# Whole transfers for the first K, the first wq pair, the last dwq pair and the last dV and dK, and a four-rows-a-partition layout for the last wo and dwo

## The chip, the cores and the metric

The kernel runs on one core of a Trainium2 chip. The metric is device time in microseconds (us), the median of several runs. The core has a matrix engine (TensorE, PE in the profile; its weight loads are PEld), a vector engine (VectorE, DVE), a scalar engine (ScalarE, ACT), GpSimd (POOL) and SyncE (SP), which here only issues transfers. Sixteen DMA engines move all data between the device memory and the on-chip memory, whose 128 rows are called partitions.

## What is computed

The forward pass is one decode step, and the kernel returns its output and the gradients of all its inputs but one:

```
q = (x @ wq) per head (32 heads of 128);  s = q . K / sqrt(128);  p = softmax(s)
a = (p @ V, heads side by side) @ wo
h = x @ w1 + b1;  b = (h * tanh(softplus(h))) @ w2
out = g * a + (1 - g) * b,   g = sigmoid(sum(x * gate_w))
returned: out, dx, dK, dV, dwq, dwo, dw1, db1, dw2, dgate_w     (for a given grad_out)
```

x has 640 elements, K and V are 32 x 4096 x 128, wq is 640 x 4096, wo is 4096 x 640, w1 is 640 x 1728, w2 is 1728 x 640, all in bf16. For each head, dV is the outer product of p with the gradient of that head's output, and dK the outer product of ds with the scaled q. So 64 MB of K and V are read, and as much of dK and dV is written.

## The kernel before

The work is a loop over the 32 heads, in groups of four (G = 4, NG = 8 groups). One head's K is one tile of 128 partitions x 32 rows x 128 elements: each partition holds 32 consecutive rows of the cache, 8192 bytes that lie together in device memory. Per head the kernel transposes K and V on TensorE (`k_tr`, `v_tr`, L504, with ScalarE copying the result at L505), computes the scores and dP (L510), the softmax (`softmax`, `exps`, `probs`), the two sums for dq and o (`dq_o`, L592), and on VectorE the two outer products into `o_sb` tiles (`outer`, L569), four of which rotate. `dv_out` and `dk_out` call `out_pair`, which issues the 1 MB store of such a tile at L582. For the last head (h = H - 1) `out_pair` stores each half of a tile as soon as it is computed (L580).

Per group there is more: the group's rows of wq (`q` needs them, and dx) and of wo (needed for the gradient of the heads' outputs, and for a), and their gradients dwq and dwo, which are written into the same tiles as the weights and stored. The tile `wq_p` holds a pair of groups, 640 rows as 128 partitions x 5 x 1024 columns. Loaded in one transfer (`load_wqp`, L130) its pieces are 2048 bytes, loaded by one group (`load_wqh`, L126) they are 1024 bytes. Before, the first pair is loaded as two halves, around the other first loads, and the last pair's dwq is stored as two halves (`f_dwq_st`, L369); the pairs between go whole (L130, L372).

The tile `wo_g` holds a group's 512 rows of wo. For groups 0 to 6 partition p holds the rows 4p to 4p+3 (`wo4_v`), 5120 bytes that lie together. There the heads' output has to be brought into that order: `f_diag` builds `o_sel` (L287), `f_o4` multiplies it with a selection matrix on TensorE (L298) and copies the result (L299, L300), and only then can a's part (`f_aT_pe`) and dwo (`f_dwo`, L376) be computed, for the whole group at once. On the way in, `g_dodiag` spreads the column by one instruction (L269), `g_dobc` broadcasts it, and `g_docol` turns the row into columns by four small matmuls (L240). For the last group (LG = 7) the layout is `wo_v`: partition d holds row d of each of the four heads, four pieces of 1280 bytes. No reordering is needed there, and each head stands by itself, so that after the loop dwo of the first three heads is computed and stored early (`f_dwo_st(g, 0, 3)`, L382), and that of head 31 later.

What sets the order: the kernel is scheduled by hand, so each engine runs its instructions in the order of the code. SP issues all large loads and stores in one stream, from one queue. The transfers of SP and of ScalarE's queue share eight semaphores; an issue on one of them waits for the transfer that had that semaphore before. In front of the loop SP issues first K (its first half), wq of group 0, K's second half, wo of group 0, V of head 0, K 1, V 1, K 2, wq of group 1, wo of group 1, V 2, K 3, w1, w2. In the loop each head issues the stores of dK of the head before and of its own dV, and the loads of K four and V three heads ahead. Behind the loop stand the last head, dK of head 30, dwo, dwq, dV of head 31, the small outputs from ScalarE's and GpSimd's queues (L842 to L844), and dK of head 31 last.

Of the kernel before, what the change touches and what calls it, by code (L numbers as in the profile page):

```python
# [7 lines left out]
ACT = mybir.ActivationFunctionType  # L8
ALU = mybir.AluOpType
AX = mybir.AxisListType  # L10
F32 = mybir.dt.float32
BF16 = mybir.dt.bfloat16
# [4 lines left out]
def kernel(  # L17
# [24 lines left out]
    nc = tc.nc  # L42
    P = 128
    _, H, Sk, Dh = A_k_cache.shape
# [3 lines left out]
    J = Sk // P  # L48
    RC = D // P
    G = 4  # L50
    NG = H // G
    GD = G * Dh
# [7 lines left out]
    scale = float(Dh) ** -0.5  # L60
    TB = 8
    NTB = J // TB
    JH = J // 2
    W = 32

    Kv = A_k_cache.rearrange("b h (p j) d -> (b h) p j d", p=P)
# [2 lines left out]
    dVv = out_3.rearrange("b h (p j) d -> (b h) p j d", p=P)  # L69
    wq_v = A_wq.rearrange("(rc r) c -> r rc c", r=P)  # L70
    dwq_v = out_4.rearrange("(rc r) c -> r rc c", r=P)
    wo_v = A_wo.rearrange("(h d) n -> d h n", d=P)
    dwo_v = out_5.rearrange("(h d) n -> d h n", d=P)
    wo4_v = A_wo.rearrange("(g p t) n -> g p t n", p=P, t=4)
    dwo4_v = out_5.rearrange("(g p t) n -> g p t n", p=P, t=4)
    assert G == 4 and NG % 2 == 0
    LG = NG - 1
    w1_v = B_w1.rearrange("(rc r) f -> r rc f", r=P)
    dw1_v = out_6.rearrange("(rc r) f -> r rc f", r=P)
    w2_v = B_w2[0:FM, :].rearrange("(p fc) n -> p fc n", p=P)  # L80
# [14 lines left out]
    kv_in = ctx.enter_context(tc.tile_pool(name="kv_in", bufs=KBUFS))  # L95
# [10 lines left out]
    kts, vts, wqs, wos = {}, {}, {}, {}  # L106

    def load_k(h):
        if h < H:
            kts[h] = kv_in.tile([P, J, Dh], BF16, name="Kn", tag="Kn")  # L110
            nc.sync.dma_start(kts[h][:], Kv[h])
# [5 lines left out]

    wqp = {}

    def wq_pair(k):  # L120
        wqp[k] = wts.tile([P, RC, 2 * GD], BF16, name="wq_p", tag="wq_p", bufs=2)
        for i in range(2):
            wqs[2 * k + i] = wqp[k][:, :, i * GD:(i + 1) * GD]

    def load_wqh(g):
        nc.sync.dma_start(wqs[g], wq_v[:, :, g * GD:(g + 1) * GD])  # L126

    def load_wqp(k):
        wq_pair(k)
        nc.sync.dma_start(wqp[k][:], wq_v[:, :, 2 * k * GD:2 * (k + 1) * GD])  # L130

    def load_wo(g):
        wos[g] = wts.tile([P, G, D], BF16, name="wo_g", tag="wo_g")
        nc.sync.dma_start(wos[g][:], wo4_v[g] if g < LG else wo_v[:, g * G:(g + 1) * G, :])

    vec_rows = const.tile([3 * RC, P], BF16, name="vec_rows")
    nc.scalar.dma_start(vec_rows[0:RC, :], x_rows)
# [1 line left out]
    nc.scalar.dma_start(vec_rows[2 * RC:3 * RC, :], gw_rows)  # L139
    dy_sb = const.tile([1, D], BF16, name="dy_sb")  # L140
    nc.scalar.dma_start(dy_sb[:], dy_row)
    kts[0] = kv_in.tile([P, J, Dh], BF16, name="Kn", tag="Kn")
    for c in range(2):
        nc.sync.dma_start(kts[0][:, c * JH:(c + 1) * JH, :], Kv[0][:, c * JH:(c + 1) * JH, :])
        if c:
            load_wo(0)
        else:
            wq_pair(0)
            load_wqh(0)
    load_v(0)  # L150
    load_k(1)
    load_v(1)
    load_k(2)
    load_wqh(1)
    load_wo(1)
    load_v(2)
    load_k(3)
# [30 lines left out]
    aT_acc = const.tile([P, RC], F32, name="aT_acc")  # L188
# [4 lines left out]
    qz, doz, p4b, ds4b = [], [], [], []  # L193
# [38 lines left out]
        nc.vector.tensor_copy(qz[g % 2][:, :, J - 1], ps[:])  # L232

    def g_docol(g):
        if g == LG:
            nc.vector.tensor_copy(doz[g % 2][:, :, J - 1], groups[g]["do_col"][:])
            return
        ps = grp([P, G], F32, "doc_ps")
        for hh in range(G):
            nc.tensor.matmul(ps[:, hh:hh + 1], lhsT=groups[g]["do_row"][0:1, hh * Dh:(hh + 1) * Dh],  # L240
                             rhs=ones_bf[0:1, 0:1], start=True, stop=True)
        nc.vector.tensor_copy(doz[g % 2][:, :, J - 1], ps[:])
# [7 lines left out]
    def g_diag(src, sc, a, b):  # L250
        diag = grp_sb.tile([P, G, P], BF16, name="diag", tag="diag")
        for hh in range(a, b):
            nc.vector.tensor_scalar(diag[:, hh, :], ident_bf[:], src[:, hh:hh + 1], sc, ALU.mult, ALU.mult)
        return diag
# [7 lines left out]

    def g_dodiag(g):
        gp = groups[g]
        if g == LG:
            gp["do_diag"] = g_diag(gp["do_col"], 1.0, 0, G)
            return
        gp["do_diag"] = grp_sb.tile([P, G, P], BF16, name="diag", tag="diag")
        nc.vector.tensor_tensor(gp["do_diag"][:].rearrange("p h d -> p (h d)").rearrange("p (k t) -> p k t", t=4),  # L269
                                ident_bf[:].unsqueeze(2).to_broadcast([P, P, 4]),  # L270
                                gp["do_col"][:].unsqueeze(1).to_broadcast([P, P, 4]), ALU.mult)

    def g_dobc(g):
        g_bcast(groups[g]["do_diag"], groups[g]["do_row"], 0, G)
# [5 lines left out]

    def f_diag(g, a=0, b=G):
        gp = groups[g]
        if g == LG:
            nc.vector.tensor_copy(gp["o_bf"][:, a:b], gp["dqo"][:, 1, a:b])
        else:
            gp["o_sel"] = grp_sb.tile([P, G, P // 4], F32, name="o_sel", tag="o_sel")
            nc.vector.tensor_tensor(gp["o_sel"][:], seg[:].unsqueeze(1).to_broadcast([P, G, P // 4]),  # L287
                                    gp["dqo"][:, 1, :].unsqueeze(2).to_broadcast([P, G, P // 4]), ALU.mult)
        gp["dq_diag"] = g_diag(gp["dqo"][:, 0, :], scale, a, b)

    def f_bc(g, a=0, b=G):
        g_bcast(groups[g]["dq_diag"], groups[g]["dq_bc"], a, b)

    def f_o4(g):
        gp = groups[g]
        gp["o4"] = grp_sb.tile([P, G], F32, name="o4", tag="o4")
        ps = grp([P, G], F32, "o4_ps")
        nc.tensor.matmul(ps[:], lhsT=gp["o_sel"][:].rearrange("p h k -> p (h k)"), rhs=res[:], start=True, stop=True)  # L298
        nc.vector.tensor_copy(gp["o4"][:], ps[:])  # L299
        nc.vector.tensor_copy(gp["o_bf"][:], gp["o4"][:])  # L300
# [37 lines left out]
    def l_dqbf(a, b):  # L338
        gp = groups[NG - 1]
        nc.vector.tensor_scalar(gp["dq_bf"][:, a:b], gp["dqo"][:, 0, a:b], scale, None, ALU.mult)  # L340

    def l_pe(a, b):
        gp = groups[NG - 1]
        gp["ax"] = grp([P, 2, RC], F32, "ax_ps")
        for i in range(2):
            for c in range(RC):
                for hh in range(a, b):
                    nc.tensor.matmul(gp["ax"][:, i, c:c + 1],
                                     lhsT=wqT[0][:, hh * RC + c, :] if i else wos[NG - 1][:, hh, c * P:(c + 1) * P],
                                     rhs=gp["dq_bf" if i else "o_bf"][:, hh:hh + 1],  # L350
                                     start=(hh == a), stop=(hh == b - 1))

    def l_add(slot):
        ax = groups[NG - 1]["ax"]
        nc.vector.tensor_tensor(aT_acc[:], aT_acc[:], ax[:, 0, :], ALU.add)
        nc.vector.tensor_copy(dx_parts[:, :, slot], ax[:, 1, :])

    def l_dwq(c, a, b):
# [6 lines left out]
        nc.vector.tensor_scalar(wqs[g][:, c, cs], groups[g]["dq_bc"][:, cs], x_col_f[:, c:c + 1], None, ALU.mult)  # L365

    def f_dwq_st(g):
        if g >= NG - 2:
            nc.sync.dma_start(dwq_v[:, :, g * GD:(g + 1) * GD], wqs[g])  # L369
        elif g % 2:  # L370
            k = g // 2
            nc.sync.dma_start(dwq_v[:, :, 2 * k * GD:2 * (k + 1) * GD], wqp[k][:])  # L372

    def f_dwo(g, hh):
        o = groups[g]["dqo"][:, 1, :] if g == LG else groups[g]["o4"][:]
        nc.scalar.activation(wos[g][:, hh, :], da_bc[:], ACT.Copy, scale=o[:, hh:hh + 1])  # L376

    def f_dwo_st(g, a=0, b=G):
        if g < LG:
            nc.sync.dma_start(dwo4_v[g], wos[g][:])  # L380
        else:
            nc.sync.dma_start(dwo_v[:, g * G + a:g * G + b, :], wos[g][:, a:b, :])  # L382

    h_sb = const.tile([P, FCN], F32, name="h_sb")
    u_sb = const.tile([P, FCN], F32, name="u_sb")
# [188 lines left out]
    def out_pair(h, dst, col4, row):  # L574
        hh = h % G
        t = outs.tile([P, J, Dh], BF16, name="o_sb", tag="o_sb")
        for a in (0, JH):
            outer(t, col4, row[:, hh * Dh:(hh + 1) * Dh], a, a + JH)
            if h == H - 1:
                nc.sync.dma_start(dst[h][:, a:a + JH, :], t[:, a:a + JH, :])  # L580
        if h < H - 1:
            nc.sync.dma_start(dst[h], t[:])  # L582

    def dv_out(h):
        out_pair(h, dVv, p4s[h], groups[h // G]["do_row"])
# [95 lines left out]
    for h in range(H - 1):  # L681
# [7 lines left out]
        v_tr(h, 2)  # L689
        v_tr(h, 3)  # L690
        exps(h, negM)
        if hh == 0 and g == LG:
            g_dobc(g)
        dP(h)
        if hh == 0 and pv:
            f_o4(g - 1)
# [62 lines left out]
        if hh == 3:  # L759
            if g % 2 == 0 and g + 2 < NG:  # L760
                load_wqp(g // 2 + 1)
            if g + 2 < NG:
                load_wo(g + 2)
            if nx:
                if g + 1 < LG:
                    g_dobc(g + 1)
                g_q(g + 1)
                g_qs(g + 1)
                g_docol(g + 1)
                f_new(g)  # L770
                f_diag(g)
            budget = 2.7
# [26 lines left out]
    dk_out(h - 1)  # L799
    od = dq_o(h)  # L800
    l_add(g)
    for i in range(3):
        f_dwo(g, i)
    f_dwo_st(g, 0, 3)
    dqo_red(h, od)
    f_diag(g, 3, 4)
    l_dqbf(3, 4)
    f_bc(g, 3, 4)
    l_pe(3, 4)
    for c in range(RC):  # L810
# [1 line left out]
    for c in range(RC):  # L812
        l_dwq(c, 3, 4)
    f_dwq_st(g)
    f_dwo(g, 3)
    f_dwo_st(g, 3, 4)
    l_add(NG)
    fin = const.tile([P, 3 * RC], F32, name="fin")
    nc.vector.scalar_tensor_tensor(fin[:, 0:RC], in0=aT_acc[:], scalar=g_all[:], in1=gb[:], op0=ALU.mult, op1=ALU.add)
# [56 lines left out]
```

## Time and profile before

| What | Value |
|---|---|
| median of 3 runs | 416.1 us (415.33 to 416.12) |
| the profiled execution | 416.13 us, its span 414.4 us |
| TensorE busy | 317.4 us (77%) |
| VectorE busy | 301.2 us (73%) |
| ScalarE busy | 215.7 us (52%) |
| moved by DMA | 165.05 MB, on the mean 398 GB/s over the span |
| packets of SP's queue | 30866, 164.05 MB |
| packets of instruction fetch (queues 8 and 14) | 66, 0.98 MB |

The span is the time from the first to the last record of the profile; 1.7 us of the execution lie outside it. A transfer is cut into packets, one for each run of bytes that lies together on both sides. A transfer over 128 partitions gives eight partitions to each of the sixteen DMA engines, and its semaphore is raised sixteen times, once by each engine when its share has landed. The trace keeps the start, size and duration of every packet, and the time of every such raise.

### The profile page before, as it was taken

The numbers are of one execution on the slowest core, as the hardware profiler recorded it, in microseconds if no ns is written. First come the engines' busy times: TensorE is split into PE (matmuls) and PEld (weight loads), VectorE is DVE, ScalarE is ACT, GpSimd is POOL, SyncE is SP. The second block draws the span as 40 slices with busy tenths as digits, with TensorE's granted clock in tenths as the row PEclk, the third lists the DMA queues.
The fourth block names the chain that finished last, engine by engine and source line by source line (L and its number), as shares of the span: only waits on it lengthen the run. The fifth ranks groups of instructions, "written<-read, shape, count | busy, mean of one in ns | idle before, by whom it ended". The sixth has DMA issues, their size and how long they took to land.

```text
span 414.4 us, 15457 instructions
## 1 busy us (share of the span) xinstructions
PE 317.4 (77%) x6839; PEld 285.2 (69%) x6839; DVE 301.2 (73%) x811; ACT 215.7 (52%) x447; POOL 10.4 (3%) x27
## 2 busy tenths in 40 slices
PE   4697995979859988888987876787978687879400
PEld 3497874878758886878777865777778685878400
DVE  2555872888689696999898885749899996886720
ACT  2364553755446445564567654774656445546600
POOL 3000001000000000000000002000000000000000
PEclk9998998989969798898989998987989898689855
DMA  8999999999999999999999999999999999999694
GB/s 273 406 413 422 419 422 422 407 420 419 421 421 420 418 419 421 411 420 419 422 420 423 416 404 411 409 417 423 422 416 375 411 394 414 403 391 377 278 346 168
DMA packets 31240, 165.05 MB, mean 398 GB/s; under 512 B 3012, under 2 KB 6725, under 8 KB 15174
## 3 DMA queue, kind: packets, MB, share of 16 engines
q1 hardware_dynamic: 30866, 164.05, 97.3%
q8 instruction: 53, 0.87, 0.8%
q14 instruction: 13, 0.11, 0.1%
q0 software_dynamic: 256, 0.01, 0.0%
q10 hardware_dynamic: 52, 0.01, 0.0%
HBM read 82.03 MB, written 82.03 MB: 396 GB/s over the span
## 4 chain that ended last, share of the span: by engine, by line
PE 32%; DMA 30%; DVE 17%; ACT 13%; issue 4%; DVEq 0%; ACTq 0%; SPq 0%
PE tr L504 14%; DMA out_dram<-o_sb 13%; DMA Vn<-in_A_v_cache_dram 10%; PE od L592 7%; DVE o_sb L569 6%; ACT KT L505 6%; DMA out_dram<-wo_g 5%; ACT VT L505 4%; PE DP L510 2%; PE S L510 2%; DVE junk L464 2%; PE q_ps L218 2%; DMA h_sb<-dh_bc 1%; DMA Kn<-in_A_k_cache_dram 1%; DVE junk L247 1%
## 5 line engine op out<-in xcount | busy, mean ns | idle before, releaser
L505 ACT COPY KT<-tr 128x512 f32<-128x512 f32 x128 | 69.8, 588 | 54.2 <-PE tr L504 54.1
L504 PE MATMUL tr<-ident_bf,Vn 128*128 128x128 bf16 x1024 | 80.3, 239 | 17.8 <-ACT VT L505 12.5
L504 PEld LDWEIGHTS <-Vn 128*128 128x128 bf16 x1024 | 71.8, 108 | 25.5 <-issue 20.1
L569 DVE TENSOR_TENSOR o_sb<-qs_row,ds 128x2048 bf16<-128x2048 bf16 x64 | 75.3, 1217 | 17.1 <-DMA out_dram<-o_sb 17.1
L505 ACT COPY VT<-tr 128x512 f32<-128x512 f32 x128 | 69.6, 584 | 27.4 <-PE tr L504 26.9
L504 PE MATMUL tr<-ident_bf,Kn 128*128 128x128 bf16 x1024 | 75.7, 230 | 7.0 <-DMA Kn<-in_A_k_cache_dram 5.5
L504 PEld LDWEIGHTS <-Kn 128*128 128x128 bf16 x1024 | 68.1, 105 | 12.0 <-DMA Kn<-in_A_k_cache_dram 5.5
L569 DVE TENSOR_TENSOR o_sb<-do_row,p 128x2048 bf16<-128x2048 bf16 x64 | 75.2, 1216 | 0.0
L532 ACT ACTIVATE dgm<-ident_bf,m 128x128 f32<-128x128 bf16 x32 | 12.9, 402 | 57.1 <-DVE m L530 57.1
L510 PE MATMUL DP<-doz,VT 128*128 128x32 bf16 x1024 | 36.3, 178 | 4.5 <-issue 2.1
L510 PE MATMUL S<-qz,KT 128*128 128x32 bf16 x1024 | 37.1, 180 | 3.1 <-ACT KT L505 0.4
L510 PEld LDWEIGHTS <-VT 128*128 128x128 bf16 x1024 | 31.7, 97 | 7.9 <-ACT VT L505 5.1
L510 PEld LDWEIGHTS <-KT 128*128 128x128 bf16 x1024 | 32.5, 98 | 6.5 <-ACT KT L505 5.6
L592 PE MATMUL od<-p,Vn 128*128 128x32 bf16 x1024 | 31.7, 179 | 3.7 <-issue 3.7
L554 PE MATMUL mx<-zd,ones_f 128*128 128x2 f32 x64 | 12.0, 258 | 25.9 <-DVE pj L550 25.7
L592 PEld LDWEIGHTS <-Vn 128*128 128x128 bf16 x1024 | 28.7, 97 | 4.1 <-issue 4.1
L592 PE MATMUL od<-ds,Kn 128*128 128x32 bf16 x1024 | 31.3, 180 | 0.1
L554 PEld LDWEIGHTS mx<-zd,ones_f 128*128 128x128 f32 x64 | 10.0, 197 | 28.8 <-DVE pj L550 28.8
L592 PEld LDWEIGHTS <-Kn 128*128 128x128 bf16 x1024 | 28.6, 98 | 0.2 <-issue 0.2
L247 DVE SCALAR_TENSOR_TENSOR junk<-wo_g,da_bc 128x640 bf16<-128x640 bf16 x32 | 25.4, 818 | 0.0
L318 DVE SCALAR_TENSOR_TENSOR junk<-wq_p,dq_bc 128x512 bf16<-128x512 bf16 x35 | 23.4, 684 | 0.7 <-ACT dq_bc L261 0.7
L538 DVE TENSOR_REDUCE negM<-mx 128x1 f32<-128x128 f32 x32 | 9.2, 286 | 17.5 <-PE mx L536 17.4
(162 smaller groups left out, 318.4 us busy)
## 6 DMA issues: line engine op xcount, KB each, us to landing
out_dram<-o_sb SPq DMA_DIRECT2D x62, 1024.0 KB, 17.5
Vn<-in_A_v_cache_dram SPq DMA_DIRECT2D x32, 1024.0 KB, 18.6
Kn<-in_A_k_cache_dram SPq DMA_DIRECT2D x31, 1024.0 KB, 17.1
wo_g<-in_A_wo_dram SPq DMA_DIRECT2D x8, 640.0 KB, 19.2
out_dram<-wo_g SPq DMA_DIRECT2D x7, 640.0 KB, 18.3
wq_p<-in_A_wq_dram SPq DMA_DIRECT2D x3, 1280.0 KB
out_dram<-wq_p SPq DMA_DIRECT2D x3, 1280.0 KB, 21.3
w_sb<-in_B_w_dram SPq DMA_DIRECT2D x1, 2160.0 KB
```

Source lines behind the costliest of these rows:

```text
L218: nc.tensor.matmul(ps[:], lhsT=x_col_bf[:, rc:rc + 1].to_broadcast([P, P]), rhs=wqs[g][:, rc, :], start=(rc == 0), stop=(rc == RC - 1))
L247: nc.vector.scalar_tensor_tensor(junk[:], in0=wos[g][:, hh, :], scalar=1.0, in1=da_bc[:], op0=ALU.mult, op1=ALU.mult, accum_out=gp["do_col ...
L318: nc.vector.scalar_tensor_tensor(junk[:, cs], in0=wqs[g][:, c, cs], scalar=1.0, in1=gp["dq_bc"][:, cs], op0=ALU.mult, op1=ALU.mult, accum_ ...
L464: nc.vector.scalar_tensor_tensor(junk[0:n, :], in0=w2_sb[0:n, fc, :], scalar=dm[0:n, fc:fc + 1], in1=db_bc[0:n, :], op0=ALU.mult, op1=ALU. ...
L504: nc.tensor.transpose(tp[:, t, :], src[:, c * TB + t, :], ident_bf[:])
L505: nc.scalar.copy(dst[:, sl, :].rearrange("p a b -> p (a b)").bitcast(F32), tp[:].rearrange("p a b -> p (a b)").bitcast(F32))
L510: nc.tensor.matmul(out, lhsT=T[:, j, :], rhs=zrow[:, J - 1 - j:2 * J - 1 - j], start=(j == 0), stop=(j == J - 1))
L532: nc.scalar.activation(dgms[h][:], ident_bf[:], ACT.Copy, scale=m32[:])
L538: nc.vector.tensor_reduce(negM[:], mx[:, 0:P], axis=AX.X, op=ALU.max, negate=True)
L554: nc.tensor.matmul(mx[:, P:P + 2], lhsT=ones_f[:], rhs=zds[h][:], start=True, stop=True)
L569: nc.vector.tensor_tensor(dst[:, a:b, :].rearrange("p j (k t) -> p j k t", t=4), row.rearrange("p (k t) -> p k t", t=4).unsqueeze(1).to_br ...
L592: nc.tensor.matmul(out, lhsT=N[:, j, :], rhs=c4[:, 4 * j:4 * j + W], start=(j == 0), stop=(j == J - 1))
```

## The change

The first K, the first wq pair, the last dwq pair, and dV and dK of head 31 are each moved in one transfer. wo and dwo of the last group take the layout of the other groups (four consecutive rows on a partition), with the reordering that goes with it: dwo of all four heads is computed and stored once, behind the last head's sums. `load_wqh`, `wo_v`, `dwo_v` and LG are gone. For the last group `g_dobc` moves to where the other groups have it, the end of the group before.

```
+    def load_wqp(k):
         wqp[k] = wts.tile([P, RC, 2 * GD], BF16, name="wq_p", tag="wq_p", bufs=2)
...
+        nc.sync.dma_start(wqp[k][:], wq_v[:, :, 2 * k * GD:2 * (k + 1) * GD])
...
-        nc.sync.dma_start(wos[g][:], wo4_v[g] if g < LG else wo_v[:, g * G:(g + 1) * G, :])
+        nc.sync.dma_start(wos[g][:], wo4_v[g])
...
-    kts[0] = kv_in.tile([P, J, Dh], BF16, name="Kn", tag="Kn")
-    for c in range(2):
-        nc.sync.dma_start(kts[0][:, c * JH:(c + 1) * JH, :], Kv[0][:, c * JH:(c + 1) * JH, :])
-        if c:
-            load_wo(0)
-        else:
-            wq_pair(0)
-            load_wqh(0)
+    load_k(0)
+    load_wqp(0)
+    load_wo(0)
     load_v(0)
     load_k(1)
     load_v(1)
     load_k(2)
-    load_wqh(1)
     load_wo(1)
...
     def f_diag(g, a=0, b=G):
         gp = groups[g]
-        if g == LG:
-            nc.vector.tensor_copy(gp["o_bf"][:, a:b], gp["dqo"][:, 1, a:b])
-        else:
+        if b == G:
             gp["o_sel"] = ...
...
     def l_pe(a, b):
+        for c in range(RC):
+            for hh in range(a, b):
+                nc.tensor.matmul(gp["ax"][:, 1, c:c + 1], lhsT=wqT[0][:, hh * RC + c, :], rhs=gp["dq_bf"][:, hh:hh + 1], ...)
+        if b == G:
             for c in range(RC):
+                for t in range(G):
+                    nc.tensor.matmul(gp["ax"][:, 0, c:c + 1], lhsT=wos[NG - 1][:, t, c * P:(c + 1) * P], ...)
...
     def f_dwq_st(g):
-        if g >= NG - 2:
-            nc.sync.dma_start(dwq_v[:, :, g * GD:(g + 1) * GD], wqs[g])
-        elif g % 2:
+        if g % 2:
...
         for a in (0, JH):
             outer(t, col4, row[:, hh * Dh:(hh + 1) * Dh], a, a + JH)
-            if h == H - 1:
-                nc.sync.dma_start(dst[h][:, a:a + JH, :], t[:, a:a + JH, :])
-        if h < H - 1:
-            nc.sync.dma_start(dst[h], t[:])
+        nc.sync.dma_start(dst[h], t[:])
...
     l_add(g)
-    for i in range(3):
-        f_dwo(g, i)
-    f_dwo_st(g, 0, 3)
     dqo_red(h, od)
     f_diag(g, 3, 4)
     l_dqbf(3, 4)
+    f_o4(g)
     f_bc(g, 3, 4)
     l_pe(3, 4)
...
     f_dwq_st(g)
-    f_dwo(g, 3)
-    f_dwo_st(g, 3, 4)
+    for t in range(G):
+        f_dwo(g, t)
+    f_dwo_st(g)
     l_add(NG)
```

More of the change, by code (lines that the diff above doesn't have):

```diff
@@ L71 @@
     dwq_v = out_4.rearrange("(rc r) c -> r rc c", r=P)
-    wo_v = A_wo.rearrange("(h d) n -> d h n", d=P)
-    dwo_v = out_5.rearrange("(h d) n -> d h n", d=P)
     wo4_v = A_wo.rearrange("(g p t) n -> g p t n", p=P, t=4)
@@ L76 @@
     assert G == 4 and NG % 2 == 0
-    LG = NG - 1
     w1_v = B_w1.rearrange("(rc r) f -> r rc f", r=P)
@@ L118 @@
     wqp = {}
-    def wq_pair(k):
+    def load_wqp(k):
         wqp[k] = wts.tile([P, RC, 2 * GD], BF16, name="wq_p", tag="wq_p", bufs=2)
@@ L123, in wq_pair @@
             wqs[2 * k + i] = wqp[k][:, :, i * GD:(i + 1) * GD]
[L125 to L129, printed above, removed]
         nc.sync.dma_start(wqp[k][:], wq_v[:, :, 2 * k * GD:2 * (k + 1) * GD])
@@ L234, in g_docol @@
     def g_docol(g):
-        if g == LG:
-            nc.vector.tensor_copy(doz[g % 2][:, :, J - 1], groups[g]["do_col"][:])
-            return
         ps = grp([P, G], F32, "doc_ps")
@@ L264, in g_dodiag @@
         gp = groups[g]
-        if g == LG:
-            gp["do_diag"] = g_diag(gp["do_col"], 1.0, 0, G)
-            return
         gp["do_diag"] = grp_sb.tile([P, G, P], BF16, name="diag", tag="diag")
@@ L282, in f_diag @@
         gp = groups[g]
-        if g == LG:
-            nc.vector.tensor_copy(gp["o_bf"][:, a:b], gp["dqo"][:, 1, a:b])
-        else:
+        if b == G:
             gp["o_sel"] = grp_sb.tile([P, G, P // 4], F32, name="o_sel", tag="o_sel")
@@ L344, in l_pe @@
         gp["ax"] = grp([P, 2, RC], F32, "ax_ps")
-        for i in range(2):
-            for c in range(RC):
[L347 to L351, printed above, removed]
+        for c in range(RC):
+            for hh in range(a, b):
+                nc.tensor.matmul(gp["ax"][:, 1, c:c + 1], lhsT=wqT[0][:, hh * RC + c, :], rhs=gp["dq_bf"][:, hh:hh + 1],
+                                 start=(hh == a), stop=(hh == b - 1))
+        if b == G:
+            for c in range(RC):
+                for t in range(G):
+                    nc.tensor.matmul(gp["ax"][:, 0, c:c + 1], lhsT=wos[NG - 1][:, t, c * P:(c + 1) * P],
+                                     rhs=gp["o_bf"][:, t:t + 1], start=(t == 0), stop=(t == G - 1))
     def l_add(slot):
         ax = groups[NG - 1]["ax"]
-        nc.vector.tensor_tensor(aT_acc[:], aT_acc[:], ax[:, 0, :], ALU.add)
+        if slot == NG:
+            nc.vector.tensor_tensor(aT_acc[:], aT_acc[:], ax[:, 0, :], ALU.add)
         nc.vector.tensor_copy(dx_parts[:, :, slot], ax[:, 1, :])
@@ L374, in f_dwo, with f_dwo_st @@
     def f_dwo(g, hh):
[L375 to L382, printed above, removed]
+        nc.scalar.activation(wos[g][:, hh, :], da_bc[:], ACT.Copy, scale=groups[g]["o4"][:, hh:hh + 1])
+    def f_dwo_st(g):
+        nc.sync.dma_start(dwo4_v[g], wos[g][:])
     h_sb = const.tile([P, FCN], F32, name="h_sb")
@@ L691 @@
         exps(h, negM)
-        if hh == 0 and g == LG:
-            g_dobc(g)
         dP(h)
@@ L764 @@
             if nx:
-                if g + 1 < LG:
-                    g_dobc(g + 1)
+                g_dobc(g + 1)
                 g_q(g + 1)
```

## The prediction

> **What bounds the kernel.** I read the page's shares first. No compute engine is busy over 77% of the span, while the DMA row stands at 9 tenths in nearly every slice. These lines of the page say so, and that SP's queue carries nearly all of it:
>
> ```profile
> PE 317.4 (77%) x6839; PEld 285.2 (69%) x6839; DVE 301.2 (73%) x811; ACT 215.7 (52%) x447; POOL 10.4 (3%) x27
> DMA  8999999999999999999999999999999999999694
> q1 hardware_dynamic: 30866, 164.05, 97.3%
> q8 instruction: 53, 0.87, 0.8%
> ```
>
> The head and the tail are where the change acts, so next I asked for the end in short windows (columns: PE, PEld, DVE, ACT, POOL busy, granted clock, DMA share, GB/s), and for the chain of waits from 379 us on:
>
> ```profile
> 388.00:390.00 2.00, 0.45 (x11) 0.35 (x10) 1.97 (x11) 0.49 (x2) 0.00 (x0) 0.97 0.09 32
> 390.00:399.00 9.00, 0.83 (x3) 0.59 (x3) 6.31 (x17) 2.32 (x7) 0.56 (x1) 0.50 1.02 404
> 399.00:403.00 4.00, 0.00 (x0) 0.00 (x0) 0.00 (x0) 0.00 (x0) 0.00 (x0) 0.50 0.75 259
> 403.00:408.00 5.00, 0.00 (x0) 0.00 (x0) 0.00 (x0) 0.00 (x0) 0.00 (x0) 0.50 1.02 404
> 408.00:413.00 5.00, 0.00 (x0) 0.00 (x0) 0.00 (x0) 0.00 (x0) 0.00 (x0) 0.50 0.07 28
> ```
>
> ```profile
> 379.42 15.35 DMA out_dram<-o_sb
> 394.77 0.02 issue
> 394.79 1.23 DVE o_sb L569
> 396.01 1.14 DVEq L871
> ```
>
> The chain ends with VectorE at 397.2 us, but the span runs to 414.4: the last 17 us are transfers alone. In the last five of them the share is 0.07, about one sixteenth, at 28 GB/s. One DMA engine is working, and fifteen are done.
>
> That engine is found in the landings, the sixteen semaphore raises of a transfer (us):
>
> ```
> transfer            issued   first  15th    last
> K 0, first half      0.74     4.18    5.41    5.43
> K 4                 28.39    43.30   45.51   45.53
> K 16               156.78   164.74  169.61  172.29
> V 30               348.35   356.17  360.74  369.69
> dK 30              392.35   398.23  398.41  405.26
> dK 31, second half 403.74   408.37  408.54  413.45
> ```
>
> One engine falls behind as the run goes on, by 9 us at 370. Listing the last landings in order of issue, each stands after the one before by what its bytes take. From dK 30: 405.26, 406.49, 408.10, 408.49, 409.75, 410.97, 412.21, 413.45. The last five steps are 0.39 (160 KB) and 1.22 to 1.26 (512 KB), and eight packets of 4096 bytes that start 0.155 apart make 1.24. So the last engine has no gap, not even at 388 to 390 us where the others sit at a share of 0.09. **The end is the last engine's stream of packets**, plus 0.9 us to the span's end (414.36) and 1.77 outside. The instruction fetches (53 of 16 KB, 1.03 us each beside other packets) are the likeliest reason that it lags, which only affects the forecast if it changes.
>
> **The change by what this stream carries.** One packet's share of the stream is its median duration less 3.5 ns, since 4096-byte packets of 159 ns start 155 apart. In ns: 1024 bytes 42.3 (46), 1280 bytes 51.5 (55), 2048 bytes 80.5 (84), 4096 bytes 155.3, 5120 bytes 192.5 (196), 8192 bytes 305.5 (309). Each engine has a sixteenth of a transfer's packets.
> - wq and dwq: four halves of 40 packets, 160 x 42.3 = 6.77 us, become two pairs of 40, 80 x 80.5 = 6.44. **-0.33.**
> - wo and dwo of group 7: 64 x 51.5 = 3.30 become 16 x 192.5 = 3.08. **-0.22.**
> - K 0, dV 31, dK 31: 48 x 155.3 = 7.45 become 24 x 305.5 = 7.33. **-0.12.**
> - Six transfers fewer, each with one semaphore packet of 7 to 9 ns: **-0.04.**
>
> The sum is **-0.7 us**. From the profiled 416.13 that gives 415.4; the runs' median 416.1 is the same within 0.03.
>
> The bounds of this term. Low: the last engine's own steps over the wq halves were 1.82, 1.80, 1.70 and 1.61, 6.93 in all, and over whole pairs 3.33 to 3.47 where no fetch shows, so two pairs may cost 6.94 and save nothing; with the other terms at their floor the saving is some 0.3. High: by mean durations, traffic included (48.9, 57.8, 86.0, 164.7, 200.4, 316.4 ns, less 3.5), wq saves 0.66, wo 0.33 and the halves 0.23, with the semaphores 1.25 in all. I take the medians because the tail, where most of these packets run, ran at them.
>
> A fixed cost of each transfer is not in the sum, because the four half stores land 1.22 to 1.26 apart and their packets alone make 1.24. The Trainium skill, "DMA: Bandwidth & Descriptors", section "Anatomy of one DMA — SWDGE (gpsimd) path", gives some 2.0 us fixed per DMA besides its bytes (for GpSimd's path). If that stood in this stream, six fewer would save 12 us; the trace disagrees.
>
> **The head, edit by edit.** K 0's halves landed at 5.43 and 8.63 with the wq half between (7.25). Whole, K 0 lands at 5.43 + 1.3 = 6.7, the wq pair at 6.7 + 3.3 = 10.0. TensorE's first transposes (5.47) wait 1.3 longer. Its queue holds behind them the matmuls on wq (L230, 7.75), and behind those the gate's z_ps, the broadcast of dy, and all of head 0; VectorE's g_do and the first store wait for these. wq now comes at 10.0, so all this moves by about 2.5 us: da_bc to 13.2, V 0's transposes from 19.1 to 21.6, the first store from 27.94 to 30.4. What hides it is the queue: when SP issued that store, the loads before it were still to land until 40.74, and at its next store (35.58) until 48.01. The least cover is 12.4 us, against 2.5. K 0's ramp is unpriced: its first packet starts at 1.75 and its last engine lands at 5.43, 3.7 us where eight packets make 1.24, so the ramp is 2.4. If it goes with bytes, the second half costs up to 2.4 more; if it is chance which engine pays, the last one may come off as well as the first (4.18), 1.25 less. I take zero, since wq's 1024-byte packets ran at about 50 ns at once behind it, near their 46.
>
> **In the loop.** The last group's four diag instructions (0.73 in all) become one of 0.68; four doc_ps matmuls (0.16 each) and the broadcast run a head earlier. wq 1 comes with wq 0. None is on the DMA stream. The half store of dwq at 375.09 goes: the stream behind it, dV 30 and dK 29 included, is 1.7 us earlier, and dK 31's outer products, which waited for the tile of dK 29 (394.77), start sooner.
>
> **The tail.** VectorE gets o_sel (0.28) and two copies (0.16 + 0.17) and loses two casts and an add; TensorE gets one product (about 0.5 with both passes), on which o_bf, the last ax_ps and aT_acc wait, and behind them on VectorE dV 31's outer products: +0.7 us at about 389. ScalarE's four dwo pieces (0.81 each) now all follow l_dwq, ready at 391.35: dwo complete at 394.5. fin_rows behind them may slip 0.5. SP then has dwq, dwo, dV 31, dK 31, all computed by about 397. Behind the semaphores of the small outputs, which held the dwq half until 398.85, they are issued by some 401. The last engine finishes dK 30 at 405.26 - 1.7 = 403.5 and reaches dK 31 near 410. All are hidden by its backlog, with over 2 us to spare at the tightest. If that cover were gone and the other fifteen engines set the end: a transfer issued into an idle queue (dw1, 389.04) first landed at 393.56 with 24 packets of 134 ns, so it started some 1.3 us after its issue. dwq issued at 398.85 would give 400.2 + 3.3 + 1.6 + 4.9 = 410.0, against their 408.5 now: 1.5 worse, still before 412.8.
>
> **The rivals.**
> 1. Forecast: only the packets count, 415.4, its own range 415.2 to 415.9. Chance 0.50.
> 2. Larger saving: traffic widens small packets as in the means (-1.25), and the wo load's step of 2.32 us, 0.66 over its work, shrinks or K 0's ramp does too: 414.8. For it: 1024-byte packets averaged 48.9, not 46. Against: the tail's ran at 46. Chance 0.27.
> 3. Slower, the head: the 2.5 us of later compute reach the end. It decides if the queue runs dry before the first stores, that is if the 12.4 us of cover are used up. Price: 2.5 - 0.7, time 417.9. The Trainium skill's same page, in the rules for kernel authors, asks to issue early and overlap compute with the transfer; by that rule the halves help. The trace has them hidden here. Against: five times the cover. K 0's ramp by bytes (+2.4 - 0.7) ends at nearly the same time, 417.8. Chance 0.13.
> 4. Nothing gained: the last engine's other delays (some 20 us over its bare packets, steps of 0.5 to 1.6 at fetches) shift by as much as is saved: 416.1. Chance 0.09.
> 5. Each transfer pays a start of its own, as K 0 paid 2.4 us: six fewer save 14.4 besides the packets, 401.0. Against: the half stores' steps. Chance 0.01. By the skill's 2.0 us it would be 403.4.
>
> **Chances.** This kernel's measurement can tell about 0.2%, 0.83 us, from no change. Faster by more: rivals 2 and 5 and little of 1, 0.30. Within: most of 1 and rival 4, 0.55. Slower: rival 3 and some of 4, 0.15. The range runs from the forecast with K 0's luckier ramp (415.4 - 1.25), below rival 2, to short of rival 3: 414.2 to 417.2.
>
> **What would show it.** Right: the last five us again at a DMA share near 0.07, last landing near 412.8, steps of 3.3 at pairs and 2.45 at dV 31 and dK 31. First store near 30.4 with no DMA slice under 9 before 60 us. Wrong: a DMA hole between 25 and 50 us (rival 3), all sixteen engines ending together (no lag, so the tail's order counts), or a last engine with gaps behind dK 30.

## The result and the profile after

The changed kernel takes 417.2 us (median of 10 runs, 416.17 to 418.53), the one before 415.54 (10 runs, 415.25 to 416.12). The ratio is 1.0039, with a 95% interval of 1.0024 to 1.0054: slower by 1.6 us, where 0.7 us faster was forecast. 417.2 is at the top edge of the stated range. The profiled execution took 417.09 us, its span is 415.3.

The page after, in the lines that were shown of before:

```profile
PE 318.2 (77%) x6845; PEld 284.4 (68%) x6845; DVE 303.3 (73%) x808; ACT 216.1 (52%) x447; POOL 11.4 (3%) x27
DMA  8999999999999999999999999999999999999892
GB/s 289 419 417 420 421 412 419 397 360 415 421 417 354 389 412 409 414 417 420 423 418 424 421 413 425 410 420 420 420 425 419 417 399 412 419 392 400 333 381 85
q1 hardware_dynamic: 28338, 164.05, 96.9%
q8 instruction: 53, 0.87, 0.8%
```

SP's queue moves the same bytes in 2528 packets fewer, and the row of tenths is as full as before. The rate tells more than the tenths. It falls in two places where it had not: 360 GB/s in the ninth slice (83 to 93 us) and 354 in the thirteenth (125 to 135). In the page of before the same two slices have 420:

```profile
GB/s 273 406 413 422 419 422 422 407 420 419 421 421 420 418 419 421 411 420 419 422 420 423 416 404 411 409 417 423 422 416 375 411 394 414 403 391 377 278 346 168
```

The end, in windows (columns: PE, PEld, DVE, ACT, POOL busy, granted clock, DMA share, GB/s), and the chain of waits from 395 us on:

```profile
403.00:408.00 5.00, 0.00 (x0) 0.00 (x0) 0.00 (x0) 0.00 (x0) 0.00 (x0) 0.50 0.76 311
408.00:414.00 6.00, 0.00 (x0) 0.00 (x0) 0.00 (x0) 0.00 (x0) 0.00 (x0) 0.50 0.06 25
```

```profile
395.92 1.12 DVEq L838
397.04 1.13 DVE o_sb L543
```

This is as forecast: the outer products are done at 398.2, and in the last six us one DMA engine works alone. Its last landings from dK 30 on are 404.53, 407.66 (dwq pair), 409.20 (dwo), 411.63 (dV 31), 414.05 (dK 31), steps of 3.13, 1.54, 2.43 and 2.42 that hold nothing but packets.

So the loss came earlier. The last engine's landing of the same transfers in the two traces:

```
                       before    after    difference
tail of w2 (last of    40.74     39.83    -0.91
 the first loads)
V 9                   116.25    116.15    -0.11
V 11                  138.61    141.29    +2.68
V 31                  377.49    378.49    +1.00
last dK               413.45    414.05    +0.60
```

The first loads arrived 0.9 us sooner. Between them and V 31 the stream lost 1.9, and behind V 31 it won 0.4 back. In this execution the net is +0.6 us at the last landing; over all runs it is +1.6. The path between is not a straight one: at V 11 the last engine is 2.68 behind, and by V 31 it has made up 1.7 of that. Each column is one execution, and the last engine takes delays of its own in both.

### The profile page after: what moved, and what is told of

The parts are those of the page before. It is cut to its first block, busy times and chain, and to the rows that moved or that the text cites. A ratio compares the mean times of both kernels' runs of the same rounds, so it can differ in the third digit from the quotient of the medians.

```text
span 415.3 us, 15457 instructions
## 1 busy us (share of the span) xinstructions
PE 318.2 (77%) x6845; PEld 284.4 (68%) x6845; DVE 303.3 (73%) x808; ACT 216.1 (52%) x447; POOL 11.4 (3%) x27
## 4 chain that ended last, share of the span: by engine, by line
PE 30%; DMA 27%; DVE 22%; ACT 12%; issue 5%; DVEq 0%; SPq 0%; ACTq 0%
DMA out_dram<-o_sb 18%; PE tr L478 12%; DVE o_sb L543 9%; PE od L563 7%; DMA Vn<-in_A_v_cache_dram 5%; ACT KT L479 5%; ACT VT L479 4%; PE S L484 2%; PE q_ps L203 2%; PE DP L484 2%; DMA wq_p<-in_A_wq_dram 2%; DVE junk L438 2%; DVE junk L295 1%; DMA h_sb<-dh_bc 1%; ACT wo_g L353 1%
## 5 line engine op out<-in xcount | busy, mean ns | idle before, releaser
L478 PE MATMUL tr<-ident_bf,Vn 128*128 128x128 bf16 x1024 | 78.6, 235 | 17.9 <-ACT VT L479 13.7
L478 PEld LDWEIGHTS <-Vn 128*128 128x128 bf16 x1024 | 69.8, 106 | 25.5 <-issue 21.8
L543 DVE TENSOR_TENSOR o_sb<-qs_row,ds 128x2048 bf16<-128x2048 bf16 x64 | 76.7, 1239 | 9.6 <-DMA out_dram<-o_sb 9.5
L563 PEld LDWEIGHTS <-Vn 128*128 128x128 bf16 x1024 | 28.7, 97 | 5.0 <-issue 5.0
L353 ACT ACTIVATE wo_g<-da_bc,o 128x640 bf16<-128x640 bf16 x32 | 24.4, 813 | 0.0
```

Of the source, the lines that this page charges most:

```text
L478: nc.tensor.transpose(tp[:, t, :], src[:, c * TB + t, :], ident_bf[:])
L543: nc.vector.tensor_tensor(dst[:, a:b, :].rearrange("p j (k t) -> p j k t", t=4), row.rearrange("p (k t) -> p k t", t=4).unsqueeze(1).to_br ...
L563: nc.tensor.matmul(out, lhsT=N[:, j, :], rhs=c4[:, 4 * j:4 * j + W], start=(j == 0), stop=(j == J - 1))
```

## Where the stream lost it

SP's own waits lead there. Around 82 and 128 us, before and after (start, duration; each store row merges two issues, dK of the head before and the head's own dV, and the second one ends it):

```profile
67.15 9.93 SPq L582 DMA_DIRECT2D out_dram<-o_sb  x2
77.17 0.38 SPq L111 DMA_DIRECT2D Kn<-in_A_k_cache_dram  x1
...
118.68 4.51 SPq L582 DMA_DIRECT2D out_dram<-o_sb  x2
123.62 0.34 SPq L111 DMA_DIRECT2D Kn<-in_A_k_cache_dram  x1
```

```profile
71.30 11.30 SPq L553 DMA_DIRECT2D out_dram<-o_sb  x2
82.69 0.38 SPq L108 DMA_DIRECT2D Kn<-in_A_k_cache_dram  x1
...
124.28 4.51 SPq L553 DMA_DIRECT2D out_dram<-o_sb  x2
129.22 0.34 SPq L108 DMA_DIRECT2D Kn<-in_A_k_cache_dram  x1
```

The same K load goes out at 82.69 in place of 77.17, and 129.22 in place of 123.62: SP is 5.5 us behind, though the first store was only 2.3 late (30.20 for 27.94). Now take the **cover** at an issue, the time from it to the landing of the transfer issued before it, for the first engine to land and for the last:

```
issue of a store   first engine   last engine
before  76.73          6.0            9.9
before 122.84          2.4            7.8
after   82.25         -0.1            2.8
after  128.44         -0.5            2.6
```

At 82 and 128 us the quickest engine of the changed kernel had nothing left. Its next landings came 2.1 and 2.4 us later than its packets take. The V load behind (83.16 and 130.05) then landed late on all sixteen engines, by 0.5 to 1.7 us, the last one included (1.48 and 1.73). In windows, before and after:

```profile
84.00:87.00 3.00, 2.92 (x99) 2.82 (x96) 2.50 (x5) 1.39 (x4) 0.00 (x0) 1.00 1.01 415
90.00:93.00 3.00, 2.96 (x54) 2.86 (x52) 1.65 (x5) 1.45 (x4) 0.00 (x0) 0.52 1.03 426
130.00:136.00 6.00, 4.62 (x149) 4.46 (x148) 4.93 (x14) 2.91 (x5) 0.00 (x0) 0.82 1.02 418
```

```profile
84.00:87.00 3.00, 2.59 (x58) 2.32 (x56) 2.94 (x5) 2.59 (x8) 0.53 (x1) 1.00 0.99 333
90.00:93.00 3.00, 3.00 (x90) 2.89 (x91) 2.50 (x8) 1.53 (x3) 0.00 (x0) 1.00 0.97 289
130.00:136.00 6.00, 5.80 (x117) 5.42 (x113) 5.70 (x19) 4.26 (x10) 0.00 (x0) 1.00 1.00 363
```

Part of the lost rate is empty engines: from 125 to 130 us the DMA share is 0.86 where the kernel before has 1.01, and in the one us from 128 on it is 0.44 against 1.00. The window before and after:

```profile
125.00:130.00 5.00, 4.80 (x93) 4.45 (x91) 4.75 (x15) 3.50 (x8) 0.00 (x0) 1.00 1.01 421
```

```profile
125.00:130.00 5.00, 4.96 (x139) 4.86 (x137) 3.50 (x9) 2.57 (x5) 0.00 (x0) 0.54 0.86 349
```

The rest is slower packets. From 90 to 93 us the share is 0.97 at 289 GB/s, and there the slowest tenth of the 8192-byte packets took 633 ns or more each, against 316 in the same window before. So a share of 1 doesn't say that the engines move data at their full rate.

The loss cannot be shared out between the two places from this pair of traces. At 82 us the changed kernel's last engine falls behind, but at V 9 it is level again (-0.11), because the last engine of before took a delay of its own in between. The whole difference at V 11 appears at 128 us.

The theory was then: the whole first wq pair makes head 0 late, the loop up to 130 us issues more slowly than the queue drains, and with the lateness the cover ends (the **dry queue**). Its rivals: the tail costs (reordering of the last group, whole last stores), or the first transfers cost by their own shape and order.

## Experiments: which part

**The first loads as before, the rest changed**, and its mirror, **the kernel before with the changed first loads**:

```
e1:  -    load_k(0)                        e2: the reverse, in the kernel before
     -    load_wqp(0)
     -    load_wo(0)
     +    (K 0 in halves, wq 0 between them, wo 0; wq 1 behind K 2)
```

> The changed kernel with the first loads as they were before (first K and first wq pair in halves); tail and last group's layout stay changed. Late-head theory (the whole first wq pair makes head 0 some 2.3 us later, and SP's queue runs dry near 82 and 128 us): the loss goes, and the tail's saving of some 0.4 us stays: 415.0 to 415.4 against 415.54 before. Tail theory (the reordering of the last group, or the whole last stores, cost): stays near 417.2. If it lies halfway, both have a part.

> The kernel before with the changed first loads alone. Late-head theory: as slow as the changed kernel or slower by the tail's 0.4 us, 417.2 to 417.8, with fast engines' landings that jump by 2 us or more beyond their packets near 82 and 128 us. Tail theory: 415.3 to 415.6, as before.

Measured: e1 415.42 us against 415.66 of the kernel before, run beside it, ratio 0.9985 (0.9970 to 1.0001). e2 417.72, ratio 1.0040 (1.0018 to 1.0062). The whole loss is in the first loads. e2's trace has the first store at 30.28, cover of -0.5 (first engine) and 2.2 (last) at 128.8, and late landings at 82.4 (2.23 us) and 128.8 (2.06).

**The tail's two parts alone**, in the kernel before:

```
e5:  f_dwq_st stores the last pair whole; out_pair stores dV 31 and dK 31 whole
e6:  wo4_v, dwo4_v, o_sel and f_o4 for the last group too; dwq, dV, dK in halves
```

> The kernel before with only the last dwq pair and the last dV and dK stored whole; last group's layout and first loads as before. Late-head theory and the packet sum: 0.2 us less than before, 415.3, nothing else. Tail theory: some 416 to 417.

> The kernel before with only the last group's wo and dwo in the four-row layout, dwq, dV and dK stored in halves. Packet sum: 0.2 us less, 415.2 to 415.5. If the reordering behind the last head (o_sel, f_o4, four dwo pieces at the end) reached the end: 0.5 to 1.5 us more.

Measured: e5 415.45 against 415.66, ratio 0.9992 (0.9975 to 1.0010); e6 415.51 against 415.81, ratio 0.9990 (0.9981 to 1.0000). Neither shows a cost. That each saves the 0.2 us of its packets fits, but 0.2 us is less than these intervals can show.

**The two first transfers apart**, in the kernel before:

```
e3:  K 0 whole, then wq 0 (half)        e4:  K 0's first half, wq pair whole, K 0's second half
```

> The kernel before with only the first K in one transfer, ahead of the first wq half. wq 0 then lands some 1 us later than before instead of 2.4. Late-head theory: first store near 29, between the two kernels in time, 415.8 to 416.6. If only the whole wq pair costs: 415.5.

> The kernel before with only the first wq pair in one transfer, between the halves of the first K. wq lands some 1.6 us later than before. Late-head theory: first store near 29.5, 416.0 to 417.0. If only the whole K costs: 415.5.

Measured: e3 415.31 against 415.53, ratio 1.0004 (0.9987 to 1.0020); e4 415.66, ratio 1.0002 (0.9987 to 1.0017). Both expectations missed: I had spread the loss over both. Neither alone costs anything that shows, though the intervals leave room for 0.8 and 0.7 us, and together they cost 1.6 us. First stores: 29.46 and 29.14, late by 1.5 and 1.2. That is what a cover with an end would do: lateness below it is free. They seem to stand near the edge. Runs over 416.9 us are 3 of 11 in e3 and 1 of 12 in e4, and 2 of 35 in the kernel before beside them, too few to tell apart. But e4's profiled execution, the highest of its runs (417.26), ran dry at 126.6 us on the quickest engine.

## Experiments: lateness without any changed transfer, and cover without an earlier head

**Lateness alone.** The same head with three g_do instructions repeated, once and twice:

```
     -    for hh in range(G):
     -        g_do(0, hh)
e7:  +    for hh in (0, 1, 2, 0, 1, 2, 3): g_do(0, hh)
e11: +    for hh in (0, 1, 2, 0, 1, 2, 0, 1, 2, 3): g_do(0, hh)
```

> The kernel before with three of the four g_do instructions of head 0 run twice (the same values again), which holds VectorE, and with it all of head 0 and the first store, by 3 x 0.82 = 2.5 us; no transfer is changed. If the lateness of the compute is what costs: 416.5 to 418, and the queue's cover near 122 us falls from 2.4 us to about nothing, with jumps in the landings there. If the shape or order of the first transfers is what costs: 415.5, as before.

> A double dose: the kernel before with the three g_do run three times, 6 x 0.75 to 0.82 = 4.6 to 4.9 us of lateness, no transfer changed. Dry-queue theory: the first 2 us or so are covered for the last engine, what is beyond reaches the end nearly whole: first store near 32.5, time 419 to 421. If the loss did not grow with the lateness: near 417.6, as with the single dose.

Measured: e7 417.59 against 415.66, ratio 1.0040 (1.0022 to 1.0058); e11 418.88 against 415.81, ratio 1.0067 (1.0051 to 1.0083). Computing the same values again on VectorE, with every transfer as it was, costs what the change cost. So the transfers' shape is not needed for the loss. Twice the dose costs 1.7 times as much, a little less than I had expected of it (419 to 421): of 4.5 us at the first store 2.8 reach the end, of e7's 2.3 it is 1.7. With nothing visible at 1.2 and 1.5, the price does not grow evenly with the lateness, and these runs do not give a formula for it. e11's quickest engine has a cover of -1.5 at 84.4, its last engine 0.95.

**Cover alone.** The third h piece of head 3 holds ScalarE, which copies it into a row whose small transfer to `h_sb` is still under way. The row of before and after (start, duration, idle before it and what ended that), with e8 below:

```profile
67.62 0.49 ACT L404 COPY dh_bc<-h_ps 1x416 f32<-1x416 f32 x1 [4.80 <-DMA h_sb<-dh_bc]
```

```profile
72.44 0.49 ACT L378 COPY dh_bc<-h_ps 1x416 f32<-1x416 f32 x1 [5.34 <-DMA h_sb<-dh_bc]
```

```profile
66.33 0.60 ACT L378 COPY dh_bc<-h_ps 1x416 f32<-1x416 f32 x2 [1.13 <-PE h_ps L375]
```

The copies of V and K behind it wait too, and with them all of the head. e8 (changed kernel) and e9 (kernel before) spread the pieces so that none waits. The edit starts the MLP's work one head earlier, so the MLP pieces that follow can move too:

```
-    mq = [("h", i) for i in range(5)] + [("gap", 0), ...
+    mq = [("h", 0), ("h", 1), ("gap", 0)] + [("h", i) for i in range(2, 5)] + [("gap", 0), ...
-        if h >= 2:
+        if h >= 1:
             mlp_some(budget)
```

> The changed kernel, with the five h pieces of the MLP spread: two in head 1, one in head 2, two in head 3, in place of one in head 2, three in head 3, one in head 4. The third piece of one head waits for a small transfer and holds ScalarE and TensorE some 5 us at 62 to 68 us; that wait goes, and nothing else of the change is touched. Dry-queue theory (the late head costs only because the queue's cover ends near 82 and 128 us): the stores near 82 are issued some 5 us earlier, the jumps in the landings go, and the time falls from 417.2 to 415.0 to 415.6, though the head is as late as before. If the late head cost in another way (its own lost time carried to the end, or the first transfers themselves): stays near 417.

> The control: the kernel before with the same spread h pieces. Dry-queue theory: its last engine never ran dry, so the wait cost it nothing and its going gains nothing: 415.3 to 415.7. If the wait at 62 us cost time by itself: some us faster, 411 to 414.

Measured: e8 415.26 against 415.53, ratio 0.9991 (0.9980 to 1.0003); e9 415.79, ratio 1.0007 (0.9994 to 1.0020). e8's first store is as late as in the changed kernel, 30.00, and yet the loss is gone. The store that went out at 82.25 goes out at 74.87, with a cover of 7.4 on the first engine and 10.9 on the last. Its windows at the two places:

```profile
84.00:87.00 3.00, 1.59 (x35) 1.42 (x32) 2.51 (x12) 1.97 (x5) 0.00 (x0) 1.00 1.00 415
90.00:93.00 3.00, 2.90 (x45) 2.83 (x46) 1.93 (x9) 1.68 (x5) 0.00 (x0) 0.80 1.00 410
130.00:136.00 6.00, 4.69 (x109) 4.59 (x105) 2.98 (x14) 2.42 (x4) 0.00 (x0) 0.68 1.00 416
```

The control shows that the wait itself is worth nothing where the last engine keeps its cover: in e9 the store of 76.73 goes out at 73.2, and the time stays as it was.

**All together**: old first loads, changed tail, spread h pieces.

> The changed tail and layout, the first loads as before, and the spread h pieces: the most cover and the fewest packets behind the loop. Dry-queue theory with the packet sum: 0.4 us under before, 415.0 to 415.3, no better than the changed tail with the old head alone, since the last engine's queue never runs dry in either.

Measured: 415.81 against 415.81, ratio 1.0002 (0.9992 to 1.0012). The expectation of 0.4 us less missed: the interval leaves room for 0.3 at most. No version beat the kernel before by more than its interval; e1 and e6 come nearest.

The kernels side by side. The cover is the lowest between 60 and 140 us in the one profiled execution, for each of the two engines by itself; the ratio is over all runs:

```
                    first store   cover, first / last engine   ratio to before
before                 27.94         2.4 /  7.8                  1
e1 old head            28.26         2.4 /  7.7                  0.9985
e4 wq whole            29.14        -0.5 /  3.5  (run of 417.26) 1.0002
e3 K whole             29.46         0.9 /  5.6                  1.0004
e8 spread h            30.00         4.1 /  6.7                  0.9991
changed                30.20        -0.5 /  2.6                  1.0039
e7 late head           30.26        -0.5 /  3.1                  1.0040
e2 changed head        30.28        -0.5 /  2.2                  1.0040
e11 later head         32.44        -1.5 /  0.95                 1.0067
```

The time goes with the cover, not with the first store: e8 and the changed kernel have nearly the same first store, and e8 loses nothing. With e7, which makes the loss by late compute alone, this shows the cause: the first loads make the compute late, and the lateness costs because the queue runs out in the middle of the run.

Three things narrow this.

- The quickest engine's cover alone does not decide. In the kernel before it is down to 0.20 us at 383.35, and its next landing there is 1.0 late, but the last engine has 11.4 us left and its step is 2.51. The kernels that are slower over all runs have 3.1 us or less on the last engine, those that are not have 5.6 or more, and e4's slow run lies between.
- An engine can be late before its cover reaches nothing: by 1.7 us at a cover of 0.67 (e7, 82.11), by 0.2 at 1.03 (changed kernel, 124.28).
- The price of one execution does not follow. e2's profiled one ran dry at both places and took 416.32, less than the median of e2 (417.72).

## Why the prediction was wrong, by its own steps

- **The last engine's stream sets the end: right.** The last six us are one engine, and its steps are packets.
- **The sum of packets: it fits where it can be seen, and no time confirms it.** Behind V 31 the stream took 35.56 us (414.05 - 378.49) in place of 35.96 (413.45 - 377.49). Those 0.40 are what half of the wq and wo terms, two thirds of the halves' term and the semaphores gave, in one pair of executions. Over all runs e10, which keeps these savings, shows no gain. One price was uneven: 159 ns for a 4096-byte packet is that of the lone last engine at the end, while the other sizes stand with the median of the whole run. That median is 162 for this size, which would make the halves' term 0.28 in place of 0.12.
- **The head's lateness: right at the first store.** Forecast 2.5 us (30.4), measured 2.3 (30.20).
- **K 0's ramp: too dear.** The whole K 0 landed at 5.73, not 6.7, so its second half cost 0.3 us and not 1.3. The other traces with a whole K 0 agree (5.81 in e2, 5.96 in e3, 5.94 in e8). The wq pair behind it then took 3.95, not 3.3. The first loads together came 0.9 us sooner, where their packets and semaphores give 0.2.
- **The cover: this step failed.** The prediction says "The least cover is 12.4 us, against 2.5." It was read at two issues, 27.94 and 35.58, from the last engine. Read on in the same listing, it falls to 7.8 at 122.84, and for the first engine to 2.4. Up to there the heads of the kernel before (MLP pieces, the wait at 62 us) take longer than their transfers, and the queue is eaten up. I stopped where the head's edit ended, but its lateness lasts far longer: the changed kernel's stores go out 5.3 to 6.1 us late from 82 us until about 220, and only around 235 to 245, where SP's issues again wait for earlier transfers (5.27 us at 235.50 in the kernel before), does this shrink to less than 4. In place of 12.4 us of cover against 2.5 of lateness, the runs show 7.8 and 2.4 (last and first engine) against 5.6, which left 2.6 and -0.5.
- **The lateness does not stay 2.5.** At 82 us it is 5.5. TensorE's granted clock is lower on the way there: 0.77 in 60 to 75 us and 0.66 in 75 to 80, where before it was 0.89 and 1.00. On the chain of waits, q_ps took 2.15 us at 61.7, before 1.09 at 58.6. The windows before and after:

```profile
60.00:75.00 15.00, 10.34 (x145) 8.16 (x144) 6.45 (x21) 6.40 (x14) 1.49 (x3) 0.89 1.01 420
75.00:80.00 5.00, 4.79 (x133) 4.42 (x129) 4.04 (x11) 3.52 (x8) 0.53 (x1) 1.00 1.03 398
```

```profile
60.00:75.00 15.00, 9.69 (x103) 6.01 (x104) 4.55 (x13) 4.50 (x9) 1.49 (x3) 0.77 1.01 418
75.00:80.00 5.00, 4.96 (x90) 4.58 (x88) 2.20 (x11) 3.29 (x8) 0.00 (x0) 0.66 1.04 400
```

That it was this clock that stretched it is argued from the rows, not shown. The other traces fit: e7 has nearly the same clock there (0.76 and 0.68) and the same lateness, 5.4; e3, at 0.77 and 1.00, keeps its lateness (1.5 at the first store, 1.6 at this one); e4, at 0.73 and 0.80, goes from 1.2 to 3.9.
- **Rival 3 is what happened, with the wrong place and too small a chance.** It named the dry queue as the deciding point, looked for it "before the first stores", and charged 1.8 over the kernel before. The price was 1.6; the queue ran dry at 82 and 128 us. That 1.8 and 1.6 are close is luck: the rival let all of 2.5 us through and took 0.7 off, while here 5.5 us of lateness met a cover, and the 0.7 shows in no time. Its sign, a DMA hole between 25 and 50 us, did not appear.
- **The tail's lateness: hidden, as forecast**, with dK 31 issued at 402.20 and landed by the last engine from 411.63 on.

The Trainium skill, "DMA: Bandwidth & Descriptors", section "Rules for kernel authors", asks to issue a DMA early, compute, and wait late. The prediction set this aside as hidden. The runs fit the rule, and show where it has a price here: e3 and e4, whose first store is late by 1.5 and 1.2 us, lose nothing that shows, and the changed head loses 1.6 at 2.3 us.

## What to carry to other kernels

In this kernel, which is bound by DMA, lateness of the compute was free up to a point, and that point was set by the least cover of the transfer queue. Look for that least over the whole stretch in which the lateness lasts, up to where the queue again holds back its issuer, not beside the edit. Read it at each issue as the landing of the transfer before less the issue, for the quickest engine and the slowest: here the slowest set the end, and where it had more than 11 us left a dry quickest engine did no harm. Edits that show no cost alone can cost together, when each uses part of the same cover; and a wait that costs nothing today (the one at 62 us) may be what takes the cover away.

## What was not expected of the hardware

- The DMA busy share hardly falls while transfers that are under way slow down: at 289 GB/s it was 0.97, at 426 GB/s 1.03. It did fall where engines had nothing queued: 0.44 at 128 to 129 us, and 0.09 at 388 to 390 us before.
- After each dry spot the V load behind it was late on all sixteen engines, also on the last, which still had 2.6 to 2.8 us of packets: 1.48 and 1.73 us beyond its packets. This is the link from the quick engines to the end of the kernel, and why it happens is open; no run here takes it apart.
- Why one engine falls behind the fifteen others by up to 7 to 10 us in all of these kernels stays open too. The instruction fetches were named as the likeliest cause, and no experiment tried it.
